# One rewritten order table, a 32-step loop in the untaken branch, and twelve matmuls moved behind that branch, in a fused attention and feed-forward kernel on one core

## The chip, the core and the metric

The kernel runs on one core of one Trainium2 chip. The metric is the device time of one execution in microseconds (us). Before the change three timed runs gave 1256.23, 1253.8 and 1254.93 us, a median of 1254.93 us. The core's engines are named as in the profile: PE (matrix products, with PEld for its weight loads), DVE, ACT and POOL (elementwise work), SP (it issues most transfers). Each engine runs its own instructions in program order and waits for others by semaphores.

## What is computed

One tensor x of 2048 rows by 512 goes through attention with 32 query heads of width 16 that share one key and one value head, and through a gated feed-forward of width 1376; a sigmoid of one column mixes the two.

```python
scores = jnp.einsum("bhqd,bkd->bhqk", q, k) * (Dh ** -0.5)
p = _softmax(scores, axis=-1)
o = jnp.einsum("bhqk,bkd->bhqd", p, v)          # then @ wo
b = (_gelu(x @ w_gate) * (x @ w_up)) @ w_down
g = _sigmoid((x * gate_w).sum(-1, keepdims=True))
return g * a + (1 - g) * b
```

All tensors are float32. A product in the kernel is made of three: each operand is split into a high and a low part, and high by high, low by high and high by low are added.

## The kernel before

**Opening.** The rows are taken in four tiles of 512 (NTG = 4). For each, PE computes keys, values and the four query blocks (L261, L389). `post_q` writes each block's 8 heads to a DRAM scratch tensor `scr` (L297, 16 transfers from SP in all). `load_q(u)` fetches the four heads of one unit back (four transfers from `scr`, two of a shift row from `shs`). There are 32 units: row tile g, block b, half a. After the last tile PE computes the gate pass `g` and the up pass `u` of weight chunk 1, twelve matmuls each (L504), with the transposes `pv` between them.

**The branch.** A flag tells whether the scores are bounded. Every engine loads it (L694) and branches (L695). Where the bound fails, a loop of 16 blocks finds the row maxima. With this input the loop's matmuls (L713) do not occur in the trace: the branch skips them. Then come `load_q(1)` and the main phase.

**Main phase.** It is a fixed interleaving of three kinds of PE work, written out in PLAN, 78 lines of tokens:

- S or Z: one score, two matmuls of 51 rows side by side (L751), 128 keys by 512 queries for two heads, into two PSUM banks. ACT takes its exponential at once (L754). S uses two of the bank pairs in turn, Z the third. There are 1024 scores, two to a step, 16 steps to a unit.
- V with a count: so many steps of probabilities times values (`pv`, L821, eight matmul records each). A run of V between other tokens is called a visit here.
- F with a count: so many pairs of feed-forward matmuls of 64 rows (`pair_mm`, L519), one into `z`, one into `y`. H begins such a job, R ends it. T issues ACT's tanh of a gate job. S, Z, V and F differ in their order alone; DVE's and POOL's work is hung on them (`slot`, `advance`, `flush`).

A line `f:` is a feed-forward job: a gate job (24 F, gate and up pass of one chunk, then the gelu chain on DVE and ACT, L544 to L560) or a down job. A line `w:` is an output job `wo_job`: 24 F that multiply the normalized heads `oh`, `ol` of one row tile by `wo`; its terms take the blocks b = 0 to 3 in order, three F each, so the tenth F is the first that reads block 3. Two `w` lines follow each of the first three row tiles; the last tile's are at the end (L504 `wos`).

**Normalization.** When a unit's 16 steps are done, `norm` copies the accumulator (L765, L775) and puts the rest in a list `bg`: sums (L781, L784), shuffle (L778), four reciprocals (L787), product (L790), `oh` (L795), `ol` (L799). `slot` takes one from the list after every third F, after split work that is due; `wo_job` empties the list when it begins. All of it runs on DVE, in the order of emission.

Of the kernel before, what the change touches and what calls it, by code (L numbers as in the profile page):

```python
# [9 lines left out]
F32 = mybir.dt.float32  # L10
F32R = mybir.dt.float32r
# [8 lines left out]
P = 128  # L20
# [106 lines left out]
def mix_kernel(ctx, tc, xT, wq, wo, wf, out):  # L127
# [16 lines left out]
    scr = dr.tile([NTG * NB, 32, 8, TG], F32, name="scr")  # L144
    shs = dr.tile([NTG * NB, 2, 3, 4, TG], F32, name="shs")
# [109 lines left out]
    for h in range(4):  # L255
        nc.gpsimd.dma_start(shs[:, :, :, h].rearrange("g a r q -> (g a) r q"), zz[:, 0:3].bitcast(F32))
# [25 lines left out]
    def post_q(tg, b, pq, last):  # L282
        q2 = p2.tile([P, 2, TG], F32R, tag="q2", name=f"q2{tg}_{b}", bufs=3)
        i = tg * NB + b

        def bound():
            nc.vector.tensor_reduce(qmx[:, i : i + 1], pq, axis=AX, op=ALU.max, apply_absolute_value=True)

        if last:
            bound()  # L290
            nc.vector.tensor_reduce(mm2[:, 0:1], qmx, axis=AX, op=ALU.max)
            nc.vector.tensor_reduce(mm2[:, 1:2], kmx, axis=AX, op=ALU.max)
        nc.scalar.copy(q2[:, 0], pq)
        if not last:
            bound()
        nc.vector.tensor_sub(q2[:, 1], pq, q2[:, 0])
        nc.sync.dma_start(scr[i].rearrange("(t d) h q -> (d h) t q", t=2), q2.bitcast(F32))  # L297
# [62 lines left out]
    def load_qk(t, rows, a):  # L360
        for j in range(2):
            hs = slice(4 * a + j, 4 * a + 4, 2)
            nc.sync.dma_start(t[64 * j : 64 * j + 32].bitcast(F32), rows[0:32, hs])
            nc.sync.dma_start(t[64 * j + 32 : 64 * j + KR].bitcast(F32), rows[0:16, hs])

    def load_shift(u):
        gb, a = divmod(u, 2)
        for j in range(2):
            nc.sync.dma_start(Q[u][64 * j + KR : 64 * j + QK].bitcast(F32), shs[gb, a, :, j::2])

    def load_q(u):
        Q[u] = cp.tile([P, 2, TG], F32R, tag="Q", name=f"Q{u}", bufs=2)
        load_qk(Q[u], scr[u // 2], u % 2)
# [313 lines left out]
    up1 = ps_a.tile([P, TG], F32, tag="pa", name="u1")  # L687
    chain_mm(up1, weights_terms(1, 1))
    gelu(1, ps, lambda: up1)
    pro.close()  # L690
# [4 lines left out]
    with tc.If(v > 0):  # L695
        with tc.tile_pool(name="gp", bufs=1) as gp:
# [4 lines left out]
            with tc.For_i(0, NTG * NB, 1) as gb:  # L701
                for a in range(2):
# [234 lines left out]
```

## Time and profile before

| | us |
|---|---|
| median of three timed runs | 1254.93 |
| the profiled execution | 1252.53 |
| its span, first to last instruction | 1250.5 |
| opening, to the first score | 81.6 |
| main phase, to the last output job | 1153.6 |
| last output job and store | 15.3 |
| ACT busy in the main phase | 997.3 |
| DVE busy in the main phase | 447.6 |

The profile is of one execution. Its page gives each engine's busy time; its waits name who waited for whom; its timeline gives start and length of each instruction. PE's matmuls overlap, so that the distance from one start to the next, not the length shown, is what a matmul costs.

### The profile page before, as it was taken

What the parts mean: (1) busy time and instruction counts of PE and PEld (TensorE: products, weight loads), DVE (VectorE), ACT (ScalarE), POOL (GpSimd) and SP (SyncE); (2) the same over time, 40 slices, a digit from 0 to 9 for tenths busy, and PEclk for the clock granted to TensorE, in tenths of its full rate; (3) what the DMA queues carried; (4) which work ended last, traced back from release to release, by engine and by line L of the source; (5) the groups of instructions that cost most, each with busy time, mean ns of one, the idle gap of its engine ahead of it and who ended that gap; (6) DMA issues with size and microseconds to landing.
All of it is one profiled execution on the core that took longest, in us unless ns stands there. A gap on an engine that the chain in (4) does not pass through costs nothing.

```text
span 1250.5 us, 23618 instructions
## 1 busy us (share of the span) xinstructions
PE 1240.0 (99%) x9742; PEld 657.4 (53%) x9742; DVE 521.1 (42%) x844; ACT 1033.1 (83%) x1127; POOL 215.5 (17%) x265
## 2 busy tenths in 40 slices
PE   9999999999999999999999999999998999999998
PEld 6865455454555554454455554455554555554444
DVE  7862453524423342533434253242635125253334
ACT  5448888889888889888988888987886888988894
POOL 5420312112210120211230021120331011121100
PEclk9999999999999999999999999999999999999999
DMA  8540302112200211201220111110220201011000
GB/s 328 194 153 38 94 1 65 40 48 82 73 15 24 75 40 40 65 23 47 74 72 19 57 65 40 40 40 23 85 82 14 73 14 65 14 52 40 14 1 34
DMA packets 28317, 73.89 MB, mean 59 GB/s; under 512 B 4208, under 2 KB 4464, under 8 KB 28208
## 3 DMA queue, kind: packets, MB, share of 16 engines
q1 hardware_dynamic: 27664, 71.32, 17.2%
q8 instruction: 77, 1.26, 0.4%
q0 software_dynamic: 256, 0.79, 0.2%
q10 hardware_dynamic: 288, 0.26, 0.1%
q14 instruction: 32, 0.26, 0.1%
HBM read 57.41 MB, written 14.94 MB: 58 GB/s over the span
## 4 chain that ended last, share of the span: by engine, by line
PE 92%; DVE 1%; DMA 0%; SPq 0%; ACT 0%; issue 0%; DVEq 0%
PE acc L821 38%; PE s L751 23%; PE y L519 16%; PE z L519 14%; PE wos L504 1%; DVE nz L787 0%; DMA Q<-scr 0%; DVE acc L634 0%; PE wof L504 0%; DVE sq L547 0%; DVE n L778 0%; DVE gs L555 0%; DVE sq L554 0%; DVE nt L790 0%; DVE sq L548 0%; DVE hl L560 0%
## 5 line engine op out<-in xcount | busy, mean ns | idle before, releaser
L754 ACT ACTIVATE p<-s 128x1024 f32<-128x1024 f32 x1024 | 979.8, 1025 | 157.5 <-PE s L751 142.7
L821 PE MATMUL acc<-p,v 128*32 128x512 f32 x4096 | 498.1, 600 | 0.0
L751 PE MATMUL s<-Q,kp 51*128 51x512 f32 x2048 | 396.9, 421 | 1.5 <-DMA Q<-scr 1.5
L751 PEld LDWEIGHTS s<-Q,kp 51*128 51x128 f32 x2048 | 183.4, 184 | 260.5 <-ACT p L754 158.4
L821 PEld LDWEIGHTS acc<-p,v 128*32 128x32 f32 x4096 | 107.3, 109 | 235.6 <-issue 224.0
L527 POOL MEMSET mark<- 1x1 f32 x77 | 7.7, 100 | 869.8 <-PE y L519 857.7
L544 DVE COPY gs<-z 128x512 f32<-128x512 f32 x39 | 27.0, 691 | 250.8 <-PE z L519 225.9
L519 PE MATMUL z<-xh,gh 64*128 64x512 f32 x312 | 123.2, 395 | 0.0
L519 PE MATMUL y<-xh,gh 64*128 64x512 f32 x312 | 123.1, 395 | 0.0
L519 PE MATMUL z<-xl,gh 64*128 64x512 f32 x312 | 121.9, 391 | 0.0
L519 PE MATMUL y<-xh,gl 64*128 64x512 f32 x312 | 121.9, 391 | 0.0
L519 PE MATMUL y<-xl,gh 64*128 64x512 f32 x312 | 121.9, 391 | 0.0
L519 PE MATMUL z<-xh,gl 64*128 64x512 f32 x312 | 121.9, 391 | 0.0
L202 POOL TENSOR_TENSOR gl<-st,gh 128x512 fp32r<-128x512 f32 x80 | 107.0, 1355 | 60.9 <-DVE gh L201 48.7
L624 DVE SCALAR_TENSOR_TENSOR acc<-z,gc,acc 128x512 f32<-128x512 f32 x24 | 18.0, 751 | 144.2 <-PE z L519 115.3
L519 PE MATMUL z<-dh,hh 64*128 64x512 f32 x176 | 69.4, 395 | 0.0
L519 PE MATMUL y<-dh,hh 64*128 64x512 f32 x176 | 69.4, 394 | 0.0
L519 PE MATMUL y<-dl,hh 64*128 64x512 f32 x176 | 68.9, 391 | 0.0
L519 PE MATMUL z<-dh,hl 64*128 64x512 f32 x176 | 68.8, 391 | 0.0
L519 PE MATMUL z<-dl,hh 64*128 64x512 f32 x176 | 68.8, 391 | 0.0
L519 PE MATMUL y<-dh,hl 64*128 64x512 f32 x176 | 68.8, 391 | 0.0
L519 PEld LDWEIGHTS z<-xh,gh 64*128 64x128 f32 x312 | 58.1, 186 | 8.1 <-issue 1.7
(174 smaller groups left out, 1534.8 us busy)
## 6 DMA issues: line engine op xcount, KB each, us to landing
st<-wf SPq DMA_DIRECT2D x40, 768.0 KB
scr<-q SPq DMA_DIRECT2D x16, 512.0 KB
Q<-scr SPq DMA_DIRECT2D x64, 128.0 KB
Q<-scr SPq DMA_DIRECT2D x64, 64.0 KB
out<-acc SPq DMA_DIRECT2D x16, 256.0 KB
xr<-xT SPq DMA_DIRECT2D x6, 512.0 KB
xst<-xT SPq DMA_DIRECT2D x12, 256.0 KB
st<-wf SPq DMA_DIRECT2D x5, 256.0 KB
```

The lines of the kernel that those rows point to most:

```text
L202: eng_l.tensor_sub(lo, src, hi)
L504: nc.tensor.matmul(ps, a, b, start=(first and q == 0), stop=(last and q == len(terms) - 1), skip_group_check=True)
L519: mm = nc.tensor.matmul(ps, a[rs], b[rs], start=(half == 0 and q == 0), stop=(half == 1 and q == len(X) - 1), skip_group_check=True)
L527: relay = nc.gpsimd.memset(mark, 0.0).ins
L544: nc.vector.tensor_copy(gs, g)
L624: nc.vector.scalar_tensor_tensor(o, ps, w, o, op0=ALU.mult, op1=ALU.add)
L751: nc.tensor.matmul(ps[:, j * TG : (j + 1) * TG], kp[rs, kc * P : (kc + 1) * P], Q[u][rs, pr], start=True, stop=True)
L754: nc.scalar.activation(p, ps, AF.Exp, bias=0.0, scale=SCALE)
L821: nc.tensor.matmul(accp[u][32 * j : 32 * j + 32], vt[:, kc], pb[s, j // 2][:, (j % 2) * TG : (j % 2 + 1) * TG], start=(kc == 0), stop=(kc ...
```

## The change

Three edits. The table PLAN is written anew: all but a few of its 78 lines differ. Its totals are 1608 F, 512 V and 1024 scores as before, 905 S and 119 Z where there were 904 and 120. V stands in 275 visits where there were 278. `scr` and `shs` are laid out by unit (32) and no longer by block with two halves, and the untaken loop runs over 32 units with a body of half the length; `post_q` writes each block in two transfers of 64 partitions, 32 from SP in all. The up pass of chunk 1 (`u`, twelve matmuls) is issued after the branch and after `load_q(1)`; the first DVE piece of its gelu chain (`chain.pop(0)()`) before the branch.

```diff
-    "t: S",
-    "f: H F S F5 S F4 S F2 S V S F2 S F4 S F4 S F2 R S V Z S T S V3 S Z S V2 S",
+    "t: S2",
+    "f: H F6 S F3 S F3 S V S F S F5 S F3 S F3 R S V S Z T S V2 Z S V2 S",
...
-    scr = dr.tile([NTG * NB, 32, 8, TG], F32, name="scr")
-    shs = dr.tile([NTG * NB, 2, 3, 4, TG], F32, name="shs")
+    scr = dr.tile([2 * NTG * NB, 32, 4, TG], F32, name="scr")
+    shs = dr.tile([2 * NTG * NB, 3, 4, TG], F32, name="shs")
...
-        nc.sync.dma_start(scr[i].rearrange("(t d) h q -> (d h) t q", t=2), q2.bitcast(F32))
+        for a in range(2):
+            nc.sync.dma_start(scr[2 * i + a].rearrange("(t d) h q -> (d h) t q", t=2),
+                              q2[64 * a : 64 * a + 64].bitcast(F32))
...
     post_v()
-    up1 = ps_a.tile([P, TG], F32, tag="pa", name="u1")
-    chain_mm(up1, weights_terms(1, 1))
     gelu(1, ps, lambda: up1)
+    chain.pop(0)()
...
-            with tc.For_i(0, NTG * NB, 1) as gb:
-                for a in range(2):
+            with tc.For_i(0, 2 * NTG * NB, 1) as u:
...
     load_q(1)
+    up1 = ps_a.tile([P, TG], F32, tag="pa", name="u1")
+    chain_mm(up1, weights_terms(1, 1))
...
     rest()
-    chain.pop(0)()
     defer(5, gates)
```

**PE ahead of the third row tile's first output job.** The rows run from the end of the gate job that stands before it to the job's first matmul (`z<-woh,oh`). A score is two rows' count (`x2`), one V step four (`x4`). Before:

```order
L751 MATMUL s<-Q_10105,kp 128x512 x2
L821 MATMUL acc_10553<-p,v_75 32x512 x12
L751 MATMUL s<-Q_10105,kp 128x512 x6
L821 MATMUL acc_10553<-p,v_75 32x512 x8
L751 MATMUL s<-Q_10105,kp 128x512 x2
L519 MATMUL z<-woh,oh_8531 128x512
```

Now:

```order
L751 MATMUL s<-Q_9973,kp 128x512 x2
L821 MATMUL acc_10426<-p,v_75 32x512 x4
L751 MATMUL s<-Q_9973,kp 128x512 x4
L821 MATMUL acc_10426<-p,v_75 32x512 x8
L751 MATMUL s<-Q_9973,kp 128x512 x6
L821 MATMUL acc_10426<-p,v_75 32x512 x8
L751 MATMUL s<-Q_9973,kp 128x512 x4
L821 MATMUL acc_10426<-p,v_75 32x512 x8
L751 MATMUL s<-Q_9973,kp 128x512 x6
L821 MATMUL acc_10426<-p,v_75 32x512 x8
L751 MATMUL s<-Q_9973,kp 128x512 x2
L519 MATMUL z<-woh,oh_8404 128x512
```

Between the gate job's end and the output job stand 9 steps of V and 12 scores, where there were 5 and 5.

**DVE at the same place.** The rows run from the gelu chain of that gate job (`gs`, `sq`, `hh`, `hl`) to the normalized heads of block 3. Before:

```order
L544 COPY gs_10543<-z 128x512
L547 SCALAR_TENSOR_TENSOR sq_10544<-gs_10543 128x512
L548 SCALAR_TENSOR_TENSOR sq_10544<-sq_10544,gs_10543 128x512
L554 SCALAR_TENSOR_TENSOR sq_10544<-sq_10544,gs_10543 128x512
L555 SCALAR_TENSOR_TENSOR gs_10543<-y,sq_10544 128x512
L559 CAST hh_10579<-gs_10543 128x512
L560 TENSOR_TENSOR hl_10580<-gs_10543,hh_10579 128x512
L781 SCALAR_TENSOR_TENSOR nz_10073<-n_10484,mk,nz_10073 128x512
L784 SCALAR_TENSOR_TENSOR nt_10072<-n_10484,mkb,nt_10072 128x512
L778 STREAM_SHUFFLE n_10071<-nz_10073 128x512
L787 RECIPROCAL nz_10073<-n_10071 128x128 x4
L790 TENSOR_TENSOR nt_10072<-nt_10072,nz_10073 128x512
```

Now:

```order
L544 COPY gs_10416<-z 128x512
L547 SCALAR_TENSOR_TENSOR sq_10417<-gs_10416 128x512
L548 SCALAR_TENSOR_TENSOR sq_10417<-sq_10417,gs_10416 128x512
L554 SCALAR_TENSOR_TENSOR sq_10417<-sq_10417,gs_10416 128x512
L555 SCALAR_TENSOR_TENSOR gs_10416<-y,sq_10417 128x512
L559 CAST hh_10462<-gs_10416 128x512
L560 TENSOR_TENSOR hl_10463<-gs_10416,hh_10462 128x512
L781 SCALAR_TENSOR_TENSOR nz_9941<-n_10364,mk,nz_9941 128x512
L784 SCALAR_TENSOR_TENSOR nt_9940<-n_10364,mkb,nt_9940 128x512
L778 STREAM_SHUFFLE n_9939<-nz_9941 128x512
L787 RECIPROCAL nz_9941<-n_9939 128x128 x4
L790 TENSOR_TENSOR nt_9940<-nt_9940,nz_9941 128x512
```

Nothing moved on DVE here; the same chain, with `oh` and `ol` behind it, stands between the gate job's end and the output job.

**PE at the branch.** The rows run from the transposes `pv` or the last of the up pass over the branch to the first work behind it. Before:

```order
L504 MATMUL u_779<-xl_532,gh_402 128x512
L504 MATMUL u_779<-xh_531,gl_403 128x512
L694 TENSOR_LOAD flag
L695 COMPARE_AND_BRANCH
L701 COMPARE_AND_BRANCH
L701 UNCONDITIONAL_BRANCH x2
L933 BRANCH_PREFETCH_HINT
L713 MATMUL gs<-kp,gq_834 128x512 x64
L721 MATMUL pt_970<-ident,m_968 4x128 x4
L713 MATMUL gs<-kp,gq_982 128x512 x64
L721 MATMUL pt_1118<-ident,m_1116 4x128 x4
```

Now:

```order
L504 MATMUL g_770<-xh_539,gl_408 128x512
L275 MATMUL pv<-ident,vt 128x128 x4
L693 TENSOR_LOAD flag
L694 COMPARE_AND_BRANCH
L700 COMPARE_AND_BRANCH
L700 UNCONDITIONAL_BRANCH x2
L932 BRANCH_PREFETCH_HINT
L711 MATMUL gs<-kp,gq 128x512 x64
L719 MATMUL pt<-ident,m_973 4x128 x4
L700 REGISTER_ALU
L700 COMPARE_AND_BRANCH
L700 UNCONDITIONAL_BRANCH
```

The branch comes twelve matmuls earlier in PE's program, and jumps over 68 matmuls where it jumped over 136.

More of the change, by code (lines that the diff above doesn't have):

```diff
@@ L255, in mix_kernel @@
     for h in range(4):
-        nc.gpsimd.dma_start(shs[:, :, :, h].rearrange("g a r q -> (g a) r q"), zz[:, 0:3].bitcast(F32))
+        nc.gpsimd.dma_start(shs[:, :, h], zz[:, 0:3].bitcast(F32))
     def passes(ps, lh, ll, rh, rl, n, first=True, last=True):
@@ L358, in mix_kernel, with load_qk @@
     Q = {}
-    def load_qk(t, rows, a):
+    def load_qk(t, rows):
         for j in range(2):
-            hs = slice(4 * a + j, 4 * a + 4, 2)
-            nc.sync.dma_start(t[64 * j : 64 * j + 32].bitcast(F32), rows[0:32, hs])
-            nc.sync.dma_start(t[64 * j + 32 : 64 * j + KR].bitcast(F32), rows[0:16, hs])
+            nc.sync.dma_start(t[64 * j : 64 * j + 32].bitcast(F32), rows[0:32, j::2])
+            nc.sync.dma_start(t[64 * j + 32 : 64 * j + KR].bitcast(F32), rows[0:16, j::2])
     def load_shift(u):
-        gb, a = divmod(u, 2)
         for j in range(2):
-            nc.sync.dma_start(Q[u][64 * j + KR : 64 * j + QK].bitcast(F32), shs[gb, a, :, j::2])
+            nc.sync.dma_start(Q[u][64 * j + KR : 64 * j + QK].bitcast(F32), shs[u, :, j::2])
     def load_q(u):
         Q[u] = cp.tile([P, 2, TG], F32R, tag="Q", name=f"Q{u}", bufs=2)
-        load_qk(Q[u], scr[u // 2], u % 2)
+        load_qk(Q[u], scr[u])
         load_shift(u)
@@ L700, in mix_kernel @@
                 nc.sync.dma_start(kp[r : r + 1].bitcast(F32), zr)
-            with tc.For_i(0, NTG * NB, 1) as gb:
-                for a in range(2):
-                    t = gp.tile([P, 2, TG], F32R, tag="gq", name=f"gq{a}", bufs=2)
-                    load_qk(t, scr[bass.ds(gb, 1)].rearrange("o r h q -> (o r) h q"), a)
-                    mx = gp.tile([P, 4, 4, 2], F32, tag="mx", name=f"mx{a}", bufs=2)
-                    for i in range(4):
-                        for h in range(4):
-                            rs = slice(64 * (h % 2), 64 * (h % 2) + KR)
-                            for e in range(2):
-                                ps = two_banks("gs")
-                                for j in range(2):
-                                    k0 = e * 1024 + j * 512
-                                    nc.tensor.matmul(ps[:, j * 512 : (j + 1) * 512],
-                                                     t[rs, h // 2, i * P : (i + 1) * P],
-                                                     kp[rs, k0 : k0 + 512], start=True, stop=True)
-                                nc.vector.tensor_reduce(mx[:, i, h, e : e + 1], ps, axis=AX, op=ALU.max)
-                    m1 = gp.tile([P, 4, 4], F32, tag="m1", name=f"m1{a}", bufs=2)
-                    nc.vector.tensor_reduce(m1, mx, axis=AX, op=ALU.max)
-                    pt = ps_f.tile([P, TG], F32, tag="pf", name=f"pt{a}")
-                    for i in range(4):
-                        nc.tensor.transpose(pt[0:4, i * P : (i + 1) * P], m1[:, i], ident)
-                    nm = gp.tile([4, TG], F32, tag="nm", name=f"nm{a}", bufs=2)
-                    nb = gp.tile([4, 3, TG], F32R, tag="nb", name=f"nb{a}", bufs=2)
-                    nc.vector.tensor_scalar(nm, pt[0:4], -1.0, None, op0=ALU.mult)
-                    nc.vector.memset(nb[:, 2].bitcast(F32), 1.0)
-                    nc.vector.tensor_copy(nb[:, 0], nm)
-                    nc.vector.tensor_sub(nb[:, 1], nm, nb[:, 0])
-                    nc.sync.dma_start(shs[bass.ds(gb, 1), a].rearrange("o r h q -> (o h) r q"), nb.bitcast(F32))
@@ new lines, in mix_kernel @@
+            with tc.For_i(0, 2 * NTG * NB, 1) as u:
+                t = gp.tile([P, 2, TG], F32R, tag="gq", name="gq", bufs=2)
+                load_qk(t, scr[bass.ds(u, 1)].rearrange("o r h q -> (o r) h q"))
+                mx = gp.tile([P, 4, 4, 2], F32, tag="mx", name="mx", bufs=2)
+                for i in range(4):
+                    for h in range(4):
+                        rs = slice(64 * (h % 2), 64 * (h % 2) + KR)
+                        for e in range(2):
+                            ps = two_banks("gs")
+                            for j in range(2):
+                                k0 = e * 1024 + j * 512
+                                nc.tensor.matmul(ps[:, j * 512 : (j + 1) * 512],
+                                                 t[rs, h // 2, i * P : (i + 1) * P],
+                                                 kp[rs, k0 : k0 + 512], start=True, stop=True)
+                            nc.vector.tensor_reduce(mx[:, i, h, e : e + 1], ps, axis=AX, op=ALU.max)
+                m1 = gp.tile([P, 4, 4], F32, tag="m1", name="m1", bufs=2)
+                nc.vector.tensor_reduce(m1, mx, axis=AX, op=ALU.max)
+                pt = two_banks("pt")[:, 0:TG]
+                for i in range(4):
+                    nc.tensor.transpose(pt[0:4, i * P : (i + 1) * P], m1[:, i], ident)
+                nm = gp.tile([4, TG], F32, tag="nm", name="nm", bufs=2)
+                nb = gp.tile([4, 3, TG], F32R, tag="nb", name="nb", bufs=2)
+                nc.vector.tensor_scalar(nm, pt[0:4], -1.0, None, op0=ALU.mult)
+                nc.vector.memset(nb[:, 2].bitcast(F32), 1.0)
+                nc.vector.tensor_copy(nb[:, 0], nm)
+                nc.vector.tensor_sub(nb[:, 1], nm, nb[:, 0])
+                nc.sync.dma_start(shs[bass.ds(u, 1)].rearrange("o r h q -> (o h) r q"), nb.bitcast(F32))
@@ L906, in _layout @@
     ins["xT"] = x.T.reshape(NC, P, NTG, TG).transpose(2, 1, 0, 3)
-    ins["wq"] = f("A_wq").reshape(NC, P, NB, 8, DH).transpose(1, 0, 2, 4, 3).reshape(P, NC, D)
+    ins["wq"] = f("A_wq").reshape(NC, P, NB, 2, 4, DH).transpose(1, 0, 2, 3, 5, 4).reshape(P, NC, D)
     ins["wo"] = f("A_wo").reshape(NB, 2, 4, DH, D).transpose(2, 1, 3, 0, 4).reshape(P, NB, D)
```

150 rows, old and new, of the table PLAN are left out of this document.

## The prediction, made before the changed kernel ran

> **What bounds the kernel now.** I read the page first, then the windows by stage, then PE's waits.
>
> ```profile
> span 1250.5 us, 23618 instructions
> ...
> PE 1240.0 (99%) x9742; PEld 657.4 (53%) x9742; DVE 521.1 (42%) x844; ACT 1033.1 (83%) x1127; POOL 215.5 (17%) x265
> ...
> PE 92%; DVE 1%; DMA 0%; SPq 0%; ACT 0%; issue 0%; DVEq 0%
> ```
>
> PE is busy throughout and holds 92% of the chain that ended last. ACT at 83% is next. The main phase, from the windows (columns: length, then busy time and count of PE, PEld, DVE, ACT, POOL; granted clock; DMA):
>
> ```profile
> 81.60:1235.20 1153.60, 1149.63 (x9361) 587.47 (x9361) 447.64 (x717) 997.26 (x1065) 181.18 (x210) 1.00 0.15 46
> ```
>
> ACT has 156 us to spare there. PE's waits name just three, of which these two are not at the start:
>
> ```profile
> PE z L519 <- DVE oh L795: 4.0, 1, 4.0
> PE s L751 <- DMA Q<-scr: 1.5, 1, 1.5
> ```
>
> So PE's own stream sets the end, and an order can win only by what is lost in one wait of 4.0 us, by the cost of switching between kinds of matmul, and at the branch (the 1.5 us). The price of each token is read where nothing waits, from start to start:
>
> ```profile
> 304.40 0.39 PE L519 MATMUL z<-dl,hh 64*128 64x512 f32 x1
> ...
> 304.63 0.39 PE L519 MATMUL z<-dh,hl 64*128 64x512 f32 x1
> ...
> 304.87 0.40 PE L751 MATMUL s<-Q,kp 51*128 51x512 f32 x2
> 305.19 1.92 PE L821 MATMUL acc<-p,v 128*32 128x512 f32 x16
> 307.05 0.50 PE L751 MATMUL s<-Q,kp 51*128 51x512 f32 x2
> 307.39 0.39 PE L519 MATMUL y<-dh,hh 64*128 64x512 f32 x1
> ...
> 309.33 1.06 PE L821 MATMUL acc<-p,v 128*32 128x512 f32 x8
> 310.33 0.97 PE L751 MATMUL s<-Q,kp 51*128 51x512 f32 x6
> ```
>
> An F takes 0.23 us (304.40 to 304.63), a score after F 0.23. A visit of two V takes 1.86 (305.19 to 307.05), of one 1.00 (309.33 to 310.33): 0.86 for each V and 0.14 for the visit. The score ahead of a visit takes 0.32 (304.87 to 305.19), the one behind it 0.34 (307.05 to 307.39): 0.09 and 0.11 over 0.23. Each visit costs 0.34 beside its V.
>
> **The change, part by part.**
>
> *The wait at the third output job.* PE's rows there:
>
> ```profile
> 959.73 0.40 PE L519 MATMUL z<-woh,ol 64*128 64x512 f32 x1
> ...
> 964.09 0.50 PE L519 MATMUL z<-woh,oh 64*128 64x512 f32 x1 [3.96 <-DVE oh L795]
> ...
> 964.43 0.40 PE L751 MATMUL s<-Q,kp 51*128 51x512 f32 x2
> ...
> 965.25 1.93 PE L821 MATMUL acc<-p,v 128*32 128x512 f32 x8
> 967.11 0.79 PE L751 MATMUL s<-Q,kp 51*128 51x512 f32 x2
> 967.70 0.63 PE L519 MATMUL z<-woh,oh 64*128 64x512 f32 x1
> ...
> 968.13 0.63 PE L519 MATMUL z<-wol,oh 64*128 64x512 f32 x1
> ...
> 968.56 0.46 PE L751 MATMUL s<-Q,kp 51*128 51x512 f32 x2
> 968.85 0.39 PE L519 MATMUL y<-woh,ol 64*128 64x512 f32 x1
> ```
>
> The tenth F of the job was due at 959.96 and started at 964.09: 4.13 us, and 0.11 on its own length (964.43 less 964.09, less 0.23). Then PE runs slowly for 3.5 us:
>
> ```profile
> 965.20:968.70 3.50, 3.50 (x18) 1.50 (x18) 0.00 (x0) 1.45 (x2) 0.09 (x1) 0.51 0.00 0
> ```
>
> The granted clock is 0.51. A one-V visit takes 1.86 in place of 1.00, the score behind it 0.59 in place of 0.34, the next two 0.43 each in place of 0.23, the last 0.29: 0.86 + 0.25 + 0.40 + 0.06 = 1.57 us. Together the place costs 5.8 us.
>
> Will the new order wait there? DVE's rows before, from the copy that ends the gate job to the heads that PE waited for:
>
> ```profile
> 951.49 0.69 DVE L544 COPY gs<-z 128x512 f32<-128x512 f32 x1 [1.10 <-PE z L519]
> ...
> 953.36 0.69 DVE L548 SCALAR_TENSOR_TENSOR sq<-sq,gs 128x512 f32<-128x512 f32 x1
> 954.75 0.69 DVE L554 SCALAR_TENSOR_TENSOR sq<-sq,gs 128x512 f32<-128x512 f32 x1 [0.70 <-ACT sq L551]
> ...
> 957.34 0.75 DVE L781 SCALAR_TENSOR_TENSOR nz<-n,mk,nz 128x512 f32<-128x512 f32 x1
> ...
> 963.61 0.43 DVE L795 CAST oh<-nt 128x512 fp32r<-128x512 f32 x1
> ```
>
> The chain takes 12.55 us (951.49 to 964.04), and its DVE order is the same in the new kernel. PE's tenth F was due 8.47 us after 951.49. In the new order the same stretch holds 24 scores and F before that F (12 scores and 9 F, and 3 scores among the F), 9 V and 5 visits, where it held 16, 5 and 2: eight more at 0.23, four V at 0.86, three visits at 0.34, together 6.3 us, so PE comes 14.8 us after the copy. Against that the tanh between 953.36 and 954.75 may be late: the new order issues three scores ahead of it (before the T), the last about 1.5 us behind the copy's start (one V, its visit and a score between), and ACT takes one in 0.96 (979.8 us over 1024, below). With half a microsecond for a score's own length (0.50, the row at 307.05) the last two end near 3.7 us after the copy's start, and tanh follows, where it could start 2.6 us after it before (954.05). The chain then takes 13.7. PE comes 1.1 us after the heads are ready. I take the 5.8 us as gone; if DVE is still late, at most all of it stays. The first two output jobs show no wait before and have the same or more V ahead of them, so nothing is late next there.
>
> *Visits.* 278 become 275, with F, V and scores unchanged: 3 x 0.34 = 1.0 us gained. Bounds: nothing (if the three are merged at a place where PE waits anyway) and 1.0.
>
> *The branch.* The rows at it:
>
> ```profile
> 79.76 0.39 PE L504 MATMUL u<-xh,gl 128*128 128x512 f32 x1
> 81.61 0.70 PE L751 MATMUL s<-Q,kp 51*128 51x512 f32 x2 [1.46 <-DMA Q<-scr]
> ```
>
> ```profile
> L695 PEldq COMPARE_BRANCH  x1: 4046/4046/4046, 77.0 to 77.0; - x1
> L695 DVEq COMPARE_BRANCH  x1: 72/72/72, 78.7 to 78.7; - x1
> ...
>   DVE dh L201: 0.5, 1
> ```
>
> PE's sequencer runs ahead of PE and spent 4.05 us in the branch, from 77.04, of which the up pass covered all but 1.62 us (1.85 less 0.23). DVE's took 0.07 us, and DVE's next instruction waited 0.5. Now the gate pass and `pv` stand ahead in place of the up pass. If PE's branch still takes 4.05 us, its cover is four short transposes and eight matmuls in place of twelve: about 0.5 us less, a loss of 0.5. If it becomes as short as DVE's, 0.5 us stay of 1.62: a gain of 1.1. Between these ends I take a gain of 0.6, nearer to the short one, because the jump is half as long and PE's is the odd one out. [...]
>
> *More transfers.* Sixteen more issues on SP, 0.42 us each:
>
> ```profile
> 72.71 1.76 SPq L369 DMA_DIRECT2D Q<-shs  x2
> 74.59 0.42 SPq L297 DMA_DIRECT2D scr<-q  x1
> ```
>
> In the last row tile SP gets to Q0's loads about one issue later, and to `load_q(1)` two. Q0's last issue ends at 74.47, 7 us ahead of the score that reads it, so that is the cover; without it the cost would be 0.4 to 0.9 us. Bytes are unchanged. The gelu piece that goes ahead of the branch (1.4 us of DVE) delays the cast `dh` behind it, which the first down job reads much later. The loop itself is skipped. All zero.
>
> The sum: 5.8 + 1.0 + 0.6 = 7.4 us. The profiled execution would take 1252.53 - 7.4 = 1245.1 (span 1243.1). It lies 2.4 below the median of the runs shown; taken from that, 1254.93 - 7.4 = **1247.5 us**.
>
> **Rivals.**
>
> *A shorter wait stays.* If the tanh or the chain is 2 to 4 us later than I worked out, PE waits 1 to 3 us. For it: a margin of only 1.1 us. Against: 6.3 us more PE work before the F. The time is 1254.93 - 7.4 + 1 to 3, with the 1.57 of slow clock beside it if that stays: 1248.5 to 1252. [...]
>
> *ACT becomes the bound.* Its row:
>
> ```profile
> L754 ACT ACTIVATE p<-s 128x1024 f32<-128x1024 f32 x1024 | 979.8, 1025 | 157.5 <-PE s L751 142.7
> ```
>
> A score every F3 (four at 0.23, 0.93 us) feeds ACT faster than it works (0.96), and the table has 268 runs of three F where it had 240. If PE then waits for a free bank before each of the 39 gate jobs' tanh, w us each, the time is 1247.5 + 39 w: at 0.26 us it is 1257.6, slower than before by 0.2%; that is the point from which it decides. For it: the denser runs. Against: ACT was idle 157.5 us waiting for PE, and PE has no wait for ACT among its three.
>
> *The table does not cure the wait.* If DVE's chain starts later by as much as PE does, 5.8 us stay: 1254.93 - 1.6 = 1253.3, no change. Against: the chain hangs on the gate job's copy, which does not move.
>
> **How the numbers follow.** My forecast (1246.0 to 1249.0) gets 0.68, a shorter wait 0.14, no cure 0.08, ACT as the bound 0.10. Within 0.2% of 1254.93 is 1252.4 to 1257.4, about what a measurement can tell from no change. Faster: 0.68 + 0.14 = 0.82; same 0.08; slower 0.10. The range for 8 in 10 reaches from 1245.6 (branch at its best, with a run's spread) to 1252.4 (most of a shorter wait); it leaves out the last two cases.
>
> **What would show it.** PE's waits should lose the line of `oh`, and no stretch of the main phase should have a granted clock near 0.5. The main phase should be about 6.8 us shorter, the first score of it at about 81.0 us. A PE wait on `p` by the dozen would make the second rival right; a wait on `oh` at the fifth or any other output job would show that my chain is too short. I would be wrong altogether if the main phase kept its 1153.6 us with no such wait, for then the token prices do not add up.

## The result and the profile after

| | before | changed |
|---|---|---|
| median of 6 runs each, us | 1254.28 (1252.88 to 1256.23) | 1247.19 (1245.65 to 1248.06) |
| the profiled execution | 1252.53 | 1247.29 |
| its span | 1250.5 | 1245.3 |
| opening, to the first score | 81.61 | 82.18 |
| first score to the start of the last V record | 1153.07 | 1147.33 |

The ratio of the changed kernel to the one before is 0.9942, 95% interval 0.9929 to 0.9954: faster by 0.58%. The medians differ by 7.09 us, and the interval is 5.8 to 8.9 us. The experiments brought 69 more runs of the kernel before, and the median of all 75 is 1253.47; the 1254.93 on which the forecast stood was the median of three runs that happened to lie high. Five more runs of the changed kernel make a median of 1247.12 over 11, and a gain of 6.35 between these larger sets. Two executions of the kernel with the up pass moved alone (below) took 1365.63 and 4026.78 us, a slow state, and are left out of all medians and ratios.

The page of the changed kernel, the three rows that were shown of before:

```profile
span 1245.3 us, 23649 instructions
...
PE 1238.3 (99%) x9742; PEld 658.0 (53%) x9742; DVE 527.6 (42%) x844; ACT 1031.5 (83%) x1127; POOL 215.8 (17%) x265
...
PE 91%; issue 1%; DVE 0%; DMA 0%; POOL 0%; SPq 0%; POOLq 0%
```

PE is the bound as before. The main phase in the windows view (length, then busy time and count of PE, PEld, DVE, ACT, POOL; clock; DMA):

```profile
82.20:1230.00 1147.80, 1147.34 (x9360) 587.99 (x9360) 452.30 (x717) 995.73 (x1065) 183.26 (x211) 1.00 0.15 47
```

It is 5.74 us shorter by the starts in the table. PE's waits (engine, line, releaser; total, times, longest):

```profile
PE gf L389 <- DVE xl L202: 0.8, 1, 0.8
PE s L751 <- DVEq L694: 0.5, 1, 0.5
PE z L519 <- POOL xl L202: 0.2, 1, 0.2
```

The line of `oh` is gone, and so is the one of `Q<-scr`; three others have come. At the third output job, DVE's chain in the timeline:

```profile
952.97 0.69 DVE L544 COPY gs<-z 128x512 f32<-128x512 f32 x1 [1.11 <-PE z L519]
...
957.18 0.69 DVE L554 SCALAR_TENSOR_TENSOR sq<-sq,gs 128x512 f32<-128x512 f32 x1 [1.65 <-ACT sq L551]
...
966.04 0.43 DVE L795 CAST oh<-nt 128x512 fp32r<-128x512 f32 x1
```

PE there, its ninth and tenth F, and the same stretch by windows:

```profile
967.27 0.39 PE L519 MATMUL z<-woh,ol 64*128 64x512 f32 x1
...
967.73 0.39 PE L519 MATMUL z<-woh,oh 64*128 64x512 f32 x1
```

```profile
965.00:969.00 4.00, 4.00 (x38) 2.94 (x38) 2.09 (x4) 4.00 (x6) 0.09 (x1) 1.00 0.00 0
```

The chain takes 13.50 us from the copy (966.47 less 952.97), PE comes 14.76 behind it, 1.26 us to spare, and the clock stays at 1.00. At the branch:

```profile
L694 PEldq COMPARE_BRANCH  x1: 352/352/352, 76.1 to 76.1; - x1
...
L694 SPq COMPARE_BRANCH  x1: 50/50/50, 80.8 to 80.8; - x1
L694 DVEq COMPARE_BRANCH  x1: 72/72/72, 81.5 to 81.5; - x1
...
  PE s L751: 0.5, 1
```

PE's branch takes 0.35 us where it took 4.05. Now DVE is the last to pass (81.5, before 78.7), and the first score waits for it. From the start of the transposes `pv` to the first score it is 4.19 us (77.99 to 82.18) where it was 4.81 (76.80 to 81.61).

Two losses are new. The first is in the gate job that opens the third row tile to be multiplied; PE stops at the F that read the low part of the reloaded x:

```profile
626.02 0.40 PE L519 MATMUL z<-xh,gh 64*128 64x512 f32 x1
...
626.50 0.49 PE L519 MATMUL z<-xl,gh 64*128 64x512 f32 x1
...
627.30 0.40 PE L519 MATMUL z<-xh,gh 64*128 64x512 f32 x1
...
627.94 0.49 PE L519 MATMUL z<-xl,gh 64*128 64x512 f32 x1 [0.23 <-POOL xl L202]
```

The steps of 0.48 and 0.64 should be 0.23 each; with 0.1 on the length of each F that restarts, that is 0.87 us. The second is in the opening, in code that the change leaves alone. Of DVE before, and then of DVE and of POOL now, the timeline has:

```profile
40.14 0.67 DVE L202 TENSOR_TENSOR xl<-xr,xh 128x512 fp32r<-128x512 f32 x1
```

```profile
40.63 3.02 DVE L202 TENSOR_TENSOR xl<-xr,xh 128x512 fp32r<-128x512 f32 x1
```

```profile
40.50 1.36 POOL L416 TENSOR_TENSOR hl<-gsf,hh 96x512 fp32r<-96x512 f32 x1
41.82 1.28 POOL L202 TENSOR_TENSOR dl<-st,dh 128x512 fp32r<-128x512 f32 x1
```

The same subtraction takes 3.02 us when the first of POOL's two begins just ahead of it, and PE gets to `pv` 1.2 us later (77.99 against 76.80). So the profiled executions differ by only 5.24 us: that of before had no such loss, that of the changed kernel had it.

### The profile page after: what moved, and what is told of

Same layout as the page of the kernel before. It is cut to its first block, busy times and chain, and to the rows that moved or that the text cites. A ratio compares the mean times of both kernels' runs of the same rounds, so it can differ in the third digit from the quotient of the medians.

```text
span 1245.3 us, 23649 instructions
## 1 busy us (share of the span) xinstructions
PE 1238.3 (99%) x9742; PEld 658.0 (53%) x9742; DVE 527.6 (42%) x844; ACT 1031.5 (83%) x1127; POOL 215.8 (17%) x265
## 3 DMA queue, kind: packets, MB, share of 16 engines
q8 instruction: 77, 1.26, 0.4%
## 4 chain that ended last, share of the span: by engine, by line
PE 91%; issue 1%; DVE 0%; DMA 0%; POOL 0%; SPq 0%; POOLq 0%
PE acc L821 38%; PE s L751 23%; PE y L519 16%; PE z L519 13%; PE wos L504 1%; DMA st<-wf 0%; POOL xl L202 0%; DVE acc L634 0%; PE wof L504 0%; SPq L369 0%; DVE dh L201 0%; SPq L365 0%; SPq L364 0%; DVE gh L201 0%; DVE gs L544 0%
## 5 line engine op out<-in xcount | busy, mean ns | idle before, releaser
L519 PEld LDWEIGHTS y<-xh,gl 64*128 64x128 f32 x312 | 57.7, 185 | 8.5
```

Source lines behind the costliest of these rows:

```text
L519: mm = nc.tensor.matmul(ps, a[rs], b[rs], start=(half == 0 and q == 0), stop=(half == 1 and q == len(X) - 1), skip_group_check=True)
```

## The experiments

All were compared with runs of the kernel before on the same chip; ratios are to those.

### The table alone, and the two other edits alone

The first takes only the new PLAN into the kernel before, the second puts the old PLAN into the changed kernel.

> Before with the new table and nothing else. My theory: the table carries the gain of the main phase, 5.8 us for the wait and the slow clock at the third output job and 1.0 for three visits, less 1.1 for small new waits seen in the changed kernel (0.66 on POOL's xl at 626 to 628 us, some 0.4 at 93 us), so 5.7 us: a median near 1248.6 where before has 1254.3, a main phase of about 1147.4 us, and PE's branch row still near 4.05 us. Rival: the branch and the unit-wise writes carry more than the 0.6 us that the traces show; then the table alone gives clearly less than 5.7, 1249.5 or more. Second rival: the table carries all of the 7.1 us between the medians; then 1247.2.

> The changed kernel with the old table, so the other two edits alone. My theory: PE's branch row falls to about 0.35 us and the stretch from pv to the first score from 4.81 to about 4.2 us, a gain of 0.6; the wait on oh and the granted clock near 0.5 at the third output job come back whole. A median near 1253.7. Rival: the DVE subtraction xl that took 3.0 us at 40.6 in the changed kernel (0.67 before) belongs to the unit-wise writes and costs the opening 1.1 us in every run; then no gain or a loss, 1254.3 to 1254.8. Second rival: these edits give the 1.4 us that the table does not explain: 1252.9.

The table alone: 1246.97 us, ratio 0.9942 (0.9929 to 0.9955). The other two edits alone: 1253.04 us, ratio 0.9996 (0.9987 to 1.0005). The table alone is as fast as the whole change. Its waits and its main phase (waits, then windows):

```profile
PE s L751 <- DMA Q<-scr: 0.9, 1, 0.9
PE z L519 <- POOL xl L202: 0.2, 1, 0.2
```

```profile
81.05:1228.30 1147.25, 1146.88 (x9361) 589.25 (x9361) 450.68 (x717) 995.55 (x1065) 182.32 (x211) 1.00 0.15 47
```

From the first score (81.04) to the last V record (1227.76) it is 1146.73 us, 6.34 less than before, and the wait on `xl` belongs to the table. In the second kernel the wait on `oh` is back:

```profile
PE z L519 <- DVE oh L795: 4.0, 1, 4.0
...
PE s L751 <- DVEq L694: 0.5, 1, 0.5
```

PE's branch row is 0.35 us there and `pv` to first score 4.19, as in the changed kernel. By the runs the two other edits can't be told from nothing. By the traces they are worth what the branch is worth (the main phase of this kernel, 1153.16 us, is as before), and that is less than one profile of before showed. In the five profiles of this study that have the old branch behind the up pass, that row took 4.05, 3.43, 3.69, 3.53 and 3.89 us, and `pv` to first score 4.81, 4.20, 4.51, 4.31 and 4.74: on average 4.51, 0.32 more than the new 4.19, and between 0.01 and 0.62 more in the single one.

### The wait at the third output job, cured, halved and made longer

Three kernels are the one before with a line or two of the old table altered. Cured by moving a job:

```diff
+    "f: H F6 S F3 S V S F2 S F4 S F3 R S V Z S2 V3 S",
     "w: H F4 S F4 S F2 S F2 V S F2 S F4 S F4 S F2 R S V S Z S V3 S Z S V3 S",
     "w: H F S F5 S F3 S F3 S V3 S F2 S F4 S F4 S F2 R S V2 S2",
-    "f: H F6 S F3 S V S F2 S F4 S F3 R S V Z S2 V3 S",
```

> Before with one line of the table moved: the feed-forward job that follows the third pair of output jobs is played ahead of them, with its own scores and V. My theory: PE comes to the tenth F of the third output job some 10 us after the heads are ready, so the wait of 4.1 us and the 1.57 us of slow clock both vanish and nothing else changes: 5.8 us, a median near 1248.5, granted clock 1.00 over the main phase. Rival: the heads slide with the job, or the wait turns up at another F or score; then 0 to 3 us are gained. Second rival: the slow clock comes from something other than this wait and stays; then 4.2 us are gained, 1250.1.

Measured 1249.83 us, ratio 0.9964 (0.9951 to 0.9976): by the ratio 4.5 us are gained of the 5.8, between the medians 3.6. By the trace the main phase is 3.48 shorter. The wait on `oh` is gone and the clock stays full, but the moved lines meet DVE and ACT in other places, two of which PE's waits name:

```profile
PE acc L821 <- DVE n L765: 0.8, 1, 0.8
PE s L751 <- ACT p L754: 0.7, 1, 0.7
```

With their restarts these take 1.9 us, and a third place 0.3. Added to the 3.48 that makes 5.7 us: the size of the term is confirmed in this profile, and also that an order which cures one wait makes others.

Shorter by one V and one score:

```diff
-    "w: H F4 S F4 S F2 S F2 V S F2 S F4 S F4 S F2 R S V S Z S V3 S Z S V3 S",
+    "w: H F4 S V S F4 S F2 S F4 S F4 S F4 S F2 R S V S Z S V3 S Z S V3 S",
```

> Before with one V and one score of the third output job played ahead of its second group of F and not behind the tenth: PE comes 1.43 us later to the tenth F, so the wait on oh is 2.7 us where it was 4.13. If the slow clock needs an idle longer than that, the granted clock stays at 1.00 behind it and 1.43 + 1.57 = 3.0 us are gained, a median near 1250.4. If any idle of some microseconds brings it, the stretch at 0.51 stays and 1.43 are gained, 1252.0. If the heads come later too, nothing is gained.

Measured 1251.29 us, ratio 0.9986 (0.9977 to 0.9996). The row of the tenth F, and the window behind it:

```profile
964.57 0.49 PE L519 MATMUL z<-woh,oh 64*128 64x512 f32 x1 [2.47 <-DVE oh L795]
```

```profile
965.20:968.60 3.40, 3.12 (x28) 2.29 (x26) 0.04 (x1) 2.36 (x3) 0.09 (x1) 1.00 0.00 0
```

In the profiled execution the clock stayed full, and the main phase was 2.45 us shorter (3.0 less 0.57 of a new wait on POOL's `mark`). But the 11 runs spread from 1250.69 to 1255.30, and the gain is 1.8 by the ratio (0.5 to 2.9), 2.4 between the medians. By the mean clock that is on record for each run, at least eight of the eleven had a slow stretch somewhere (last section); the profiled execution is one of the other three.

Longer, by two V and a score:

```diff
-    "... R S V3 T S Z S V2 S",
-    "w: H F4 S F4 S F2 S F2 V S F2 ...",
+    "... R S V3 T S Z S",
+    "w: H F4 S F4 S F2 S F2 V2 S V S F2 ...",
```

> Before with two V and a score taken from ahead of the third output job and put behind its tenth F: PE comes 2.3 us earlier and waits 6.4 us on oh. If the slow stretch has a fixed length, it stays at 3.5 us and 1.57 us lost, and the time is 2.3 us longer: 1255.7. If it grows with the idle, it lasts 5 us or more and the time is some 3 us longer: 1256.5. If the heads hang on PE's place, the wait stays at 4.1 and the time at 1253.4.

Measured 1255.95 us, ratio 1.0019 (1.0010 to 1.0029): 2.4 us longer by the ratio. In PE's timeline the job's first F now stopped for ACT, which takes the score that shares the job's banks, so that the wait on `oh` grew by only 0.4; the window shows the clock behind it:

```profile
956.85 0.49 PE L519 MATMUL z<-woh,oh 64*128 64x512 f32 x1 [1.63 <-ACT p L754]
...
964.01 0.79 PE L519 MATMUL z<-woh,oh 64*128 64x512 f32 x1 [4.33 <-DVE oh L795]
```

```profile
962.60:969.30 6.70, 5.29 (x24) 1.75 (x24) 1.98 (x4) 1.02 (x1) 0.09 (x1) 0.50 0.00 0
```

The slow stretch lasts 6.8 us here. The wait never became 6.4, so neither form of the expectation is met: what grew is one wait on ACT and a second slow stretch.

### The branch: place or length

The fourth kernel moves only the up pass behind the branch, with the old loop (136 matmuls to jump over) and the old table; the fifth only shortens the loop (68) and doubles the transfers, with the up pass ahead.

> Before with the up pass moved behind the branch as in the change, the loop of 16 blocks (136 matmuls jumped) and the old table kept. If the length of the jump makes PE's branch slow, its row stays near 4.05 us, its cover is pv and eight matmuls in place of twelve, and the time is about 0.5 us longer: 1254.8. If the place of the branch in PE's program makes it slow, the row falls to about 0.35 us and the time is about 0.6 to 1.1 us shorter: 1253.2 to 1253.7.

> Before with only the layout by unit and the loop of 32 short bodies: the up pass stays ahead of the branch, the table is the old one. What the run with the up pass moved alone showed: the branch row fell to 0.35 us, but PE then stood still 2 us behind its first matmul and ran slowly for 4, so with 136 matmuls jumped some 4 to 5 us pass between the branch and steady work wherever the branch stands. If the length of the jump decides, here the row is near 0.35 us with no stall behind it, and the first score follows the up pass by less than 0.9 us where it took 1.85: 0.5 to 1.1 us gained, a median near 1252.6 against 1253.4. If it is not the length, the row stays between 3.4 and 4.1 us and the time at 1253.4.

Up pass moved alone: 1254.68 us over ten runs, ratio 1.0008 (0.9999 to 1.0017). The branch row and, in PE's timeline, what stands behind it:

```profile
L694 PEldq COMPARE_BRANCH  x1: 353/353/353, 75.8 to 75.8; - x1
```

```profile
78.43 0.47 PE L504 MATMUL u<-xh,gh 128*128 128x512 f32 x1
80.86 0.50 PE L504 MATMUL u<-xl,gh 128*128 128x512 f32 x1 [1.96 <-issue]
```

```profile
81.40:84.70 3.30, 3.30 (x9) 2.56 (x8) 0.43 (x1) 0.00 (x0) 1.28 (x1) 0.50 0.45 114
```

The row fell as the place would have it, yet the loss did not: behind the first matmul PE stood idle for 2 us with no wait that the trace shows (`issue`), and then had half the clock for 3.4. From the branch to the second matmul it is 5.0 us (75.84 to 80.86), a time like that of the long row (4.05 before). The kernel with the old table and both edits differs from this one by the layout by unit and its short loop, and has no such stall (0.35 us of branch row, 4.19 from `pv` to the first score). That the stall came with the long jump is my reading of this pair, 68 matmuls without one and 136 with one; what PE waits for in it isn't shown. It need not lie in the branch's own row, which is 0.35 us in both. The DMA view from 75 to 86 us divides the profiles in the same way: on queue 8, which it calls `instruction`, it counts two packets of 16 KB in each of the six profiles with 136 matmuls to jump, and one in each of the eight with 68. No run tried a length between.

Short loop alone: 1254.95 us, ratio 1.0009 (1.0000 to 1.0018), no gain at all. The branch row, and PE's first score:

```profile
L695 PEldq COMPARE_BRANCH  x1: 352/352/352, 77.0 to 77.0; - x1
```

```profile
82.39 0.70 PE L750 MATMUL s<-Q,kp 51*128 51x512 f32 x2 [2.20 <-SPq L695]
```

PE was free of its branch at 77.4 and done with the up pass at 80.2, and then SP was late: at the branch it waits until the last writes to `scr` have landed (the semaphore that it stands at, to 82.0, is that of the last one). With 32 issues in place of 16 SP came to the branch at 79.5, where it came at 76.3 before. Behind the idle time of 2.2 us there was again a slow stretch (the granted clock is 0.50 from 83.2 to 86.5 us), 1.5 us lost. Whether a stall like that of the kernel above hides under this wait the trace can't tell. But the number of issues is not all of it: in the kernel with the V ahead, below, SP comes to the branch at 79.5 too, and its steps there end at 80.6, where here they end at 82.2. Why the last write landed some 1.5 us later here isn't shown. So the transfers that I costed at nothing can have a price, and what sets its size is open.

### Two cures on top of the change

In the opening, DVE's last `xl` of the second tile goes ahead of the cast `dh`; in the gate job at 624 us, one V goes ahead of the F that wait.

```diff
-            if ti == 1 and b < 3:
+            if ti == 1 and b != 2:
...
-                parts[b]()
-                if b == 2:
+                parts[min(b, 2)]()
+                if b == 3:
                     fetch_w(2)
```

```diff
-    "f: H F S F5 S F3 S F3 S V S F S F5 S F3 S F3 R S V Z S T S V4 S Z S V2 S",
+    "f: H F S V S F5 S F3 S F4 S F2 S F3 S F3 S F3 R S V Z S T S V4 S Z S V2 S",
```

> The changed kernel with two small cures. A V and a score go ahead in the gate job at 624 us, where PE waited for POOL's xl: 0.85 us. In the opening DVE makes the last xl of the second tile ahead of the cast dh, so that it doesn't meet POOL's two subtractions (3.0 us in place of 0.67 at 40.6, 1.0 us on PE in most of the profiles so far): up to 1.0 us. Both right: 1245.4. Rivals: the two engines meet at another instruction and the opening keeps its 1.0 us, 1246.3; the V moved ahead waits for the accumulator's copy and nothing is gained there, 1246.2; both, 1247.2.

Measured 1248.67 us, ratio 0.9959 (0.9946 to 0.9973): above the changed kernel's 1247.19. The opening lost nothing. The V took a score with it, and split work is deferred by a count of scores: POOL's `gl` came ahead of its `mark`. In the timelines of POOL and PE, and the window behind:

```profile
626.44 2.88 POOL L202 TENSOR_TENSOR gl<-st,gh 128x512 fp32r<-128x512 f32 x2
629.26 0.37 POOL L527 MEMSET mark<- 1x1 f32 x1
```

```profile
629.69 0.55 PE L519 MATMUL z<-xh,gh 64*128 64x512 f32 x1 [1.87 <-POOL mark L527]
```

```profile
630.00:633.40 3.40, 3.40 (x18) 2.66 (x16) 0.00 (x0) 2.05 (x2) 1.28 (x1) 0.50 0.32 76
```

Behind an idle time of 1.87 us the granted clock was 0.50. The next three ran beside each other: the opening's cure alone; with it the V alone moved, scores left behind their F as far as they can be; and the changed kernel once more.

```diff
-    "f: H F S F5 S F3 S F3 S V S F S F5 S F3 S F3 R S V Z S T S V4 S Z S V2 S",
+    "f: H F S V F5 S F3 S F3 S F2 S F2 S F2 S F3 S F3 R S V Z S T S V4 S Z S V2 S",
```

> The changed kernel with the opening's cure alone: DVE makes the last xl of the second tile ahead of the cast dh. In nine profiles so far the opening lost 1.0 us five times, three of them at this xl, and in the one profile with this edit not at all. If the place is cured, PE's first score stands near 81.1 us unless the other place (the xl of the first tile, near 10 us) loses its 1.0 us, and the median falls by 0.3 to 0.6: 1246.7. Rival: POOL and DVE meet elsewhere in the opening; 1247.2 stays.

> The same, and in the gate job at 624 us the V alone goes ahead, its scores stay behind the same F, but for the two that stood around it. The run before had moved a score too; the split work is counted in scores, so POOL's gl came ahead of its mark, and PE waited 1.9 us and ran 3.4 us at half clock. Now POOL's order is as in the changed kernel. If that was the cause, no wait on mark and no half clock stand there and the waits on xl are gone: 0.85 us less than the opening's cure alone, 1245.9. Rival: the V stops at the accumulator's copy or the mark still comes late: 1246.7 or more.

> The changed kernel once more, beside the two cures on the same chip: 1247.2, and a second profile of it. If the opening's 1.0 us is chance and no part of the change, its first score stands near 81.1 or near 82.2 us, either way with the branch row of PE at 0.35 us and the granted clock at 1.00.

| | median, us | lowest to highest | ratio to before |
|---|---|---|---|
| opening's cure | 1245.96 (5 runs) | 1245.85 to 1246.88 | 0.9941 (0.9927 to 0.9954) |
| cure and V ahead | 1245.66 (5) | 1245.46 to 1245.79 | 0.9936 (0.9922 to 0.9949) |
| changed, again | 1245.76 (5) | 1245.36 to 1247.89 | 0.9944 (0.9930 to 0.9957) |

The changed kernel's eleven runs fall into four from 1245.36 to 1245.76 and seven from 1246.98 to 1248.06; its second profile had no loss in the opening and took 1245.36. With the cure, 15 of the 16 runs of three kernels (the one below among them) lie between 1245.35 and 1246.29. The loss comes and goes from run to run. In the 14 profiles `pv` starts at 77.7 to 78.0 five times and at 76.3 to 76.9 nine times, late with both layouts of `scr`, and never late in the four (the first of these cures among them) in which the opening was altered. Three of the five lost the time at the subtraction that the cure moves, two at another `xl` near 10 us that it does not touch, so that the cure can be credited with the first kind only, and why the second kept away from these four isn't settled. The V ahead gained 0.13 us of main phase, not 0.87: the waits on `xl` went, and about 0.6 us of small stops came behind them.

### One piece of the change undone

On top of the last cure, the first piece of the gelu chain goes back behind the branch.

```diff
     gelu(1, ps, lambda: up1)
-    chain.pop(0)()
...
     rest()
+    chain.pop(0)()
```

> The kernel of the run before the last (V ahead, opening cured) with one piece of the change undone: the first DVE piece of the gelu chain stands behind the branch again. In that run the first score started 0.12 us behind DVE's last step at the branch (80.88), 0.36 behind SP's (80.64), and 0.63 later than the up pass would let it. If the gelu piece is what makes DVE late, DVE's step comes some 1.4 us earlier, the first score follows SP's at about 80.76, and 0.24 us are gained: 1245.4 against 1245.7. If DVE stays late or the two pieces then delay the cast dh or the tanh, nothing is gained or the time is longer, 1245.7 to 1246.2.

Measured 1245.61 us (1245.35 to 1245.79, 6 runs), ratio 0.9938 (0.9926 to 0.9950), against 1245.66 with the piece ahead. PE's first score with the piece ahead, and then behind:

```profile
81.00 0.82 PE L751 MATMUL s<-Q,kp 51*128 51x512 f32 x3 [0.47 <-DVEq L694]
```

```profile
80.86 1.03 PE L750 MATMUL s<-Q,kp 51*128 51x512 f32 x4 [0.32 <-DVE sq L547]
```

The first score comes 0.14 us earlier, now behind that piece itself; the medians don't tell it from nothing.

## Why the prediction was right, point by point

**The wait at the third output job: right, mechanism and size.** The chain was put at 13.7 us and took 13.50, PE was to come 14.8 behind the copy and came 14.76. The line of `oh` and the slow clock are both gone, and the table alone carries the gain. The 5.8 us are the price in the profiled execution; by the estimate from the mean clocks in the last section, 38 of 69 other runs of the kernel before had a second slow stretch of 3.4 us, so that its price there may be higher.

**Visits: right as far as it can be told.** The main phase of the table alone is 6.34 us shorter; with the 0.87 lost on `xl` added back that is 7.2, where 5.8 and 1.0 make 6.8. No run moved visits alone.

**Nothing late next: wrong.** "The first two output jobs show no wait before ... so nothing is late next there" looked at the output jobs only. The reload of x for the third row tile is due as well, and the new table leaves DVE and POOL less PE work in which to make `xl`: 0.87 us, in every profile with the new table as it stands. Add 0.35 at 93 us in the first profile, where the third score bank waited for a copy; the second profile does not have it. So the main phase gained 5.74 and 6.05 us in the two profiles, where 6.8 was forecast.

**The branch: right in direction, size too large.** PE's row fell from 4.05 to 0.35 us with the jump half as long; what makes the long one slow isn't shown. 0.6 was taken from one execution in which the old branch had its longest row of the five; the mean gain by the traces is 0.32, which the runs can't tell from nothing. Which engine ends the wait is new too: DVE.

**More transfers at zero: near in this kernel, for the wrong reason.** The cover named was the 7 us between Q0's last issue and its score. What counts is that SP passes the branch only when `scr` is written. In the changed kernel its last step there stands at 81.9, where it stood at 77.6, and DVE's at 82.1, so the first score waits for DVE with 0.2 us to spare: that the cost is near zero is luck, and the kernel with the short loop alone, where PE waits 2.2 us for SP, shows how it can go. The price of an issue was also wrong. Three rows of SP, first of before and then of the changed kernel:

```profile
56.48 0.39 SPq L421 DMA_DIRECT2D hs<-hh  x1
```

```profile
58.53 0.61 SPq L421 DMA_DIRECT2D hs<-hh  x1
...
77.78 1.36 SPq L298 DMA_DIRECT2D scr<-q  x2
```

An issue was put at 0.42 us; two of the last writes take 1.36, and even `hs`, which the change leaves alone, takes 0.61 beside 0.39.

**The gelu piece at zero: right in time.** Moved back, it changed the median by 0.05 us, though it is what makes DVE last at the branch.

**The time: near, with two errors that offset each other.** 1247.5 was 1254.93 less 7.4. The measured gain by the traces is 5.74 to 6.05 in the main phase and 0.32 at the branch, some 6.1 to 6.4, where 7.4 was forecast; the base was 1.46 above the median of 75 runs. That the two offset each other is luck.

**The rivals.** No wait for ACT's `p` appears on PE in the changed kernel's two profiles, so ACT is not the bound. (Its 157.5 us of idle time were not all for PE, as the forecast has it: the row gives 142.7 to `s`.) That the table would not cure the wait is out by the same rows. The shorter wait did not come, with 1.26 us to spare; what it would have cost was tried, and the slow clock, which the forecast adds "if that stays", came in some executions of the same kernel and not in others (below).

## What to carry to other kernels

In a hand-ordered stream, one wait of 4 us can be worth more than every saving in the order itself, and its cure is read from two numbers: when the operand is ready, and when its reader comes. Then every other deadline that the moved work used to cover has to be checked in the same way, not those of the same kind alone; the moved job and the first of the two cures both took away one wait and made another. Before a forecast of half a per cent is set against the median, see how the profiled execution stands among many runs, and whether the loss that is priced is the same size in each of them.

## What the runs showed of the hardware

**The granted clock changed on a grid of 3.41 us.** In each trace here every change of the granted clock lies at a whole multiple of 3.4133 us from the first record of it. In that of the kernel before it stands at 1.00 for 959.145 us, at 0.50 for 3.413 and at 1.00 for 279.893, which is 281, 1 and 82 of these cells, and in that of the changed kernel at 1.00 for 1239.038 us, 363 of them. Laid on that grid, with the idle time of PE worked out from the timeline and the length shown as a share of a cell:

```
run                      PE idle, us        idle share, cell by cell   granted clock
before                   960.13 to 964.09   0.51, then 0.65            half in the cell after the second
old table, other edits   960.95 to 964.92   0.38, then 0.78            half in the cell after the second
up pass moved alone      78.91 to 80.86     0.57                       half in the next cell
  the same, third job    963.59 to 967.48   0.54, then 0.60            half in the cell after the second only
short loop alone         80.19 to 82.39     0.64                       half in the next cell
  the same, third job    961.80 to 965.76   0.58, then 0.58            half in both next cells
wait shorter             962.10 to 964.57   0.49, then 0.24            full throughout
both cures               627.82 to 629.69   0.55                       half in the next cell
```

Of cells at full clock, those with 0.55 or more idle were followed by one at half clock, those with 0.54 or less were not. With every gap of PE counted, over all cells of the 14 profiles, the lowest share that was followed is 0.548 and the highest that was not is 0.536. A cell that was itself slow was followed by a second one with only 0.44 idle (the longer wait). So the clock was halved behind 1.87 us in one run and not behind 2.47 in another: in these rows it goes by where the idle time falls on the grid, and the grid's place is not the same in each run: in the 14 profiles the first record comes 4.35 to 6.78 us behind the start of the span (6.13 in the kernel before, 6.03 in the changed one). A slow cell cost 1.57 us in the profile of the kernel before.

The mean granted clock, which is on record for each run of the experiments, tells what one profile can't. By an estimate from these profiles, a slow cell takes 0.0014 from it (half of 3.41 us in 1250), and the stretch at half clock that ends a span at most 0.0008 (half of up to 1.95 us). Of the 69 further runs of the kernel before, 38 stand at 0.997, which by that takes two slow cells, and their median is 1254.12; 27 stand at 0.999, with 1252.99. The profiled one (0.998) had one. The changed kernel's runs stand at 0.999 and 1.000. Of the eleven runs with the shorter wait six stand at 0.998 and two, the slowest, at 0.997, so that at least eight had a slow cell; all ten with the longer wait stand at 0.997. Of the five with both cures, one stands at 1.000, without a slow cell, and it is the fastest (1246.93). So the same wait of some 2 us (1.87 and 2.47 in the two profiles) comes with a slow cell in some executions and without one in others, which fits the spread of these runs. It doesn't explain all of it: the fastest run with the shorter wait (1250.69) stands at 0.998. Where in the runs without a profile the slow cells lay isn't shown.

**A DVE subtraction was held up where POOL's began first.** The subtraction `xl` near 40 us took 0.67 us when it began ahead of POOL's `hl` (40.14 and 40.76 in the kernel before). It took 3.02 when `hl` began 0.13 us ahead of it; POOL's second one, `dl`, followed and ran to 43.1, and `xl` ended 0.55 behind that. All 14 profiles agree: 3.02 in the three in which POOL came first, 0.67 or 0.68 in the others. The late openings at 10 us are of the same kind: in the kernel with the two other edits alone two `xl` from 7.89 us on took 2.50 together, POOL's `gl` having begun at 8.54, just ahead of the second; in the kernel before it began at 8.80, behind it, and they took 1.38. One profile, in which the two began within 0.02 us of each other, lost nothing. Which engine comes first changed from run to run of the same kernel, and it moved the start of `pv` by 0.9 to 1.2 us.
